# Attention and gated layer in one kernel: no MoE unit in a pair's step, its first product in another PSUM bank

## The chip, the cores and the metric

One core of a Trainium2 chip runs the whole program. The metric is device time in microseconds of one execution, the median of three runs. TensorE (PE) multiplies and transposes, VectorE (DVE), ScalarE (ACT) and GpSimd (POOL) do the rest, SyncE (SP) issues nearly all transfers. Each engine works through its own instructions in the order in which they were written.

## The reference

Everything is fp32. Attention of 4 batches x 8 heads x 576 positions x 64 with rotated q and k is followed by a layer "x @ w_in, relu, a convolution of three taps along the sequence, sigmoid gate, @ w_out", called MoE in the code.

```python
q_rot, k_rot = (rotate(q), rotate(k))
scores = scale * np.matmul(q_rot, k_rot.transpose(0, 1, 3, 2))
attn = np.exp(scores - np.max(scores, axis=-1, keepdims=True))
attn = attn / (np.sum(attn, axis=-1, keepdims=True) + 1e-09)
x = np.matmul(attn, v)                      # heads side by side: 4 x 576 x 512
h = np.maximum(x @ w_in, 0.0)               # 512 -> 1024
conv_out = sum(conv_w[k] * hp[:, k:k + S, :] for k in range(3))
out = (h * (1.0 / (1.0 + np.exp(-conv_out)))) @ w_out
```

## The kernel before

The order of the work is written out by hand: every engine executes in the order in which the loop over steps `n` emits. Heads go in 16 pairs `p`; a pair takes five steps, `n = 5p + s`. In step `n`:

- **S** (`emit_S`, L251): the scores of one block of 128 query rows for both heads, into the PSUM tiles `sp` (two buffers). VectorE takes the maxima (L259), ScalarE the exponentials (L263) into `st`, or `str` for the short fifth block.
- **T** (`emit_T`, L311): the transposes of the block of the step before, into the two PSUM buffers `tp` (`t_tile`); ScalarE copies them to `pt` (L189). Blocks 0 to 3 fill columns 0 to 511 of `pt`, the fifth (10 transposes, called T4 here) columns 512 to 575.
- **R** (`emit_Trem`, L336): remaining columns, in steps `n % 5 == 2` and `4`, also in a `tp` buffer, copied by VectorE (L191).
- **E** (`emit_E`, L367): the product with V, all of it in the steps `n % 5 == 0` (called pair steps), one part per half `j`. Half 0 reads columns 0 to 289 of `pt`, half 1 columns 286 to 575. `spare` gives each a `tp` buffer; ScalarE copies it to `xn` (L377).
- `emit_rinv` (L344 to 354): reciprocal of the sums, through DRAM into `rb`; `norms` (L381) multiplies `xn` by it, then `xT` is made in two parts (L385 ScalarE, L386 GpSimd).

From step `WIDE = 26` on, MoE units are put between these. The 2304 positions are 8 blocks of 288. **M1** (`emit_M1`, 12 matmuls, L400) is one eighth of a block's first product, in a buffer of the PSUM pool `m` (two buffers, `pm`); then come relu (L408 ACT), convolution (L412, L414 DVE), tanh (L420 ACT), gate (L423 DVE), and a split in two parts (L431 ACT, L432 POOL) into `g`. `defer` puts these a number of ticks (units on PE) later. **M2** (`emit_M2`, 6 matmuls, L478) is a quarter of the second product for 128 positions; its `pm` buffer is held over four units, then VectorE copies it to `ot` (L485) and SyncE stores it (L488).

The table `moe` says which unit goes into which step. A block's units get a place x in 0 to 1; a step holds as much of that as its entry of `room` says. Before, a block has `MB = 10` steps, and a pair step has half the room of another. Transfers are in the same table: rank 19 puts `load` and `load_v` at the end of a step, behind its units, those of V (`vm`, `vr`) and of k into steps `n % 5 == 3`. After the last step two blocks are left for the tail, in which `m_tile` has other buffers.

Of the kernel before, what the change touches and what calls it, by code (L numbers as in the profile page):

```python
# [20 lines left out]
def attention_moe_kernel(ctx, tc, q, k, v, w_in, conv_w, w_out, tab, tabx, out):  # L21
# [3 lines left out]
    NP = B * NPB  # L25
# [3 lines left out]
    NF = DFF // 128  # L29
# [4 lines left out]
    STEPS = 5  # L34
# [5 lines left out]
    psum = {}  # L40
# [39 lines left out]
    def defer(k, fn, rank=1):  # L80
        due.setdefault(slot[0] + k, []).append((rank, len(due.get(slot[0] + k, [])), fn))
# [6 lines left out]
    def t_tile():  # L88
        return psum["t"].tile([128, 512], F32, tag="t", name="tp")

    def after(fn):
        if "m" in psum or late["n"] + 1 == WIDE:
            fn()
        else:
            at(late["n"] + 1, 0.35, fn)

    def spare(n):
        a = free["at"]
        if "m" in psum or late["n"] + 1 == WIDE:
            return t_tile()[:, 0:n]  # L100
        assert a + n <= 960
        free["at"] = a + n
        return free["ps"][:, a:a + n]

    def m_tile():
        if late["tail"]:
            return psum["t"].tile([128, 512], F32, tag="mt", name="mt")
        return psum["m"].tile([128, 512], F32, tag="m", name="pm")
# [131 lines left out]
    def go(d, key):  # L240
        for fn in d.pop(key):
            fn()
# [89 lines left out]
    def emit_Trem(p, first, num):  # L332
        ps = spare(128 * num)
        for u in range(num):
            x = ST[p, first + u].rearrange("p h k -> p (h k)")[:, 512:640]
            nc.tensor.transpose(ps[:, 128 * u:128 * u + 128], x, idf)  # L336
        after(lambda: evac("V", pt[:, 8, 128 * first:128 * (first + num)], ps))
# [19 lines left out]
    norms = {}  # L357
# [2 lines left out]

    def emit_E(p, j, a=0, n=XW):
        b, hp = divmod(p, NPB)
        xp = spare(n)
        o = (S - XW) * j
        for i in range(5):
            for h in range(2):
                nc.tensor.matmul(  # L367
                    out=xp[64 * h:64 * h + 64, :],
                    lhsT=vmain[p][:, h, i, :] if i < 4 else vrem[:, h, :],
                    rhs=pt[:, 2 * i + h if i < 4 else 8, o + a:o + a + n],  # L370
                    start=(i == 0),
                    stop=(i == 4),
                )
        if a == 0:
            xns[p, j] = p2.tile([128, XW], F32, tag="xn", name="xn", bufs=4)
        xn = xns[p, j]
        after(lambda: nc.scalar.activation(out=xn[:, a:a + n], in_=xp, func=AF.Copy))  # L377

        def norm():
            sl = xslot[b, hp, j] = free_slots.pop(0)  # L380
            nc.vector.tensor_tensor(out=xn, in0=xn, in1=rb[p][:, o:o + XW], op=ALU.mult)  # L381

        def split():
            sl = xslot[b, hp, j]
            nc.scalar.activation(out=xT[:, sl, 0, :], in_=xn, func=AF.Copy)  # L385
            nc.gpsimd.tensor_tensor(out=xT[:, sl, 1, :], in0=xn, in1=xT[:, sl, 0, :].bitcast(F32), op=ALU.subtract)  # L386

        norms[p, j] = lambda: (norm(), defer(1, split))
# [194 lines left out]
    def m2_units(blk):  # L583
        tiles = list(range(HS * blk // 128, HS * (blk + 1) // 128))
        return [lambda t=t, i=i: emit_M2(t, i) for t in tiles for i in range(4)]
# [8 lines left out]
    WIDE = 26  # L594
    MB = 10
# [4 lines left out]
    def at(n, rank, fn):  # L600
        plan.setdefault(n, []).append((rank, len(plan.get(n, [])), fn))

    def emit():
        with tc.manual_schedule(engines=engines):
# [17 lines left out]
            for p in range(1, NP):  # L622
                n = STEPS * p
# [6 lines left out]
            for p in range(NP):  # L630
                n = STEPS * p
                for s in range(STEPS):
                    m = n + s
                    first = m < WIDE
                    if m:
                        at(m - 1 if first else m, 0.5 if first else 0, lambda p=p, s=s: emit_S(p, s))
                    at(m, 0.2, lambda p=p, s=s: go(reds, (p, s)))
                    at(m, 0.3 if first else 1.5, lambda p=p, s=s: go(exps, (p, s)))
                    for h in range(2 if s < 4 else 1):
                        at(m + 1, 0 if m + 1 < WIDE else 1, lambda p=p, s=s, h=h: emit_T(p, s, h))  # L640
                if n + 4 < WIDE:
                    for i in range(4):
                        at(n + 1 + i, 2, lambda p=p, i=i: emit_Trem(p, i, 1))
                else:
                    for i in range(2):
                        at(n + 2 + 2 * i, 2, lambda p=p, i=i: emit_Trem(p, 2 * i, 2))
                if n + 8 < WIDE:
                    for i in range(4):
                        at(n + 5 + i, 4, lambda p=p, i=i: emit_E(p, i // 2, XW // 2 * (i % 2), XW // 2))
                else:  # L650
                    for i in range(2):
                        m = n + 5 + (i if n + 5 < WIDE else 0)
                        at(m, 4 if m < WIDE else 10, lambda p=p, i=i: emit_E(p, i))
                at(n + 5, 4.5, lambda p=p: emit_rinv(p))
                for j in range(2):
                    at(n + (9 if j and n + 8 < WIDE else 8), 1.7 + j, lambda p=p, j=j: norms.pop((p, j))())
            nw = len(wsteps)
            for i, u in enumerate(wsteps):
                x = (WIDE - 1) * i // nw
# [2 lines left out]
            at(14, 2, turn_cw)  # L662
            moe = {}
            for blk in range(2 * B - 2):
                n0 = WIDE + MB * blk
                room = [0.5 if n % STEPS == 0 and n < STEPS * NP + 2 else 1.0 for n in range(n0, n0 + MB)]
                us = [(0.09 + 0.1 * f, lambda blk=blk, f=f: emit_M1(blk, f)) for f in range(NF)]
                if blk:
                    m2 = m2_units(blk - 1)
                    ne = 4 if blk % 4 == 0 else 0  # L670
                    us += [(0.05 * i if i < ne else 0.05 * ne + (1 - 0.05 * ne) * (i - ne) / (len(m2) - ne), u) for i, u in enumerate(m2)]
                for x, u in us:
                    y, k = x * sum(room), 0
                    while y >= room[k]:
                        y -= room[k]
                        k += 1
                    moe.setdefault(n0 + k, []).append((x, u))
# [56 lines left out]
            for u in seq + second + m2_units(last) + m2_units(LASTB):  # L734
                u()
                tick()

    emit()


# [48 lines left out]
```

## Time and profile before

| what | value |
|---|---|
| three runs | 515.56, 516.81, 519.25 us; median 516.81 |
| the profiled execution | 514.66 us, of it the span 512.7 |
| PE busy | 469.0 us (91%), 3880 matmuls |
| DVE, ACT, POOL busy | 365.0 (71%), 311.8 (61%), 300.3 us (59%) |
| granted TensorE clock | 0.983 on the mean of the span; 1.00 in every stretch from 128 us on |
| chain that ended last | PE 67%, DVE 13%, ACT 7%, POOL 5%, DMA 5% |

PE is busy to nine tenths or more in nearly each slice from step 26 (about 128 us) on. A busy share of an engine does not say whether a wait of PE ends on it; this is read from the waits, step by step. A pair step can be found in the timeline of PE by its ten transposes of `str`; a step begins with eight matmuls into `sp`.

### The profile page before, as it was taken

Reading aid. Unit: us, or ns where it says so; the run is one execution under the profiler, and the core shown is the slowest. Engines: PE = TensorE matmul, PEld = TensorE weight load, DVE = VectorE, ACT = ScalarE, POOL = GpSimd, SP = SyncE. Lnnn points to the kernel's source line nnn. Section 1 sums busy time; section 2 is a strip of 40 time slices with the busy share of each in tenths; the row PEclk is TensorE's granted clock in tenths of the full one; section 3 lists DMA queues with packets and bytes.
Section 4 is the critical chain, followed back from the end, with each engine's and each line's share of the span. In section 5 each row is a group of like instructions: output and inputs, shape, how many; then the busy total and the mean of one; then the engine's idle time right before and its main releaser. Section 6 shows DMA issues by size and latency. Waiting matters only on the chain.

```text
span 512.7 us, 10801 instructions
## 1 busy us (share of the span) xinstructions
PE 469.0 (91%) x3880; PEld 350.0 (68%) x3880; DVE 365.0 (71%) x656; ACT 311.8 (61%) x821; POOL 300.3 (59%) x479
## 2 busy tenths in 40 slices
PE   1878789786999899999999999999999999999997
PEld 1445446553766587767878687868777676889986
DVE  5699889995597759684868487765868284748951
ACT  2588877885576767675667575754657564325520
POOL 3789988999576747646492829274573021314530
PEclk9999987997999999999999999999999999999999
DMA  8978965843424243433425251524220201000011
GB/s 225 178 128 165 191 158 140 188 113 76 88 47 94 47 93 68 93 69 73 90 49 90 63 100 45 88 73 88 51 68 1 68 1 46 22 21 22 1 42 60
DMA packets 139256, 42.61 MB, mean 83 GB/s; under 512 B 132012, under 2 KB 132804, under 8 KB 139204
## 3 DMA queue, kind: packets, MB, share of 16 engines
q1 hardware_dynamic: 137860, 41.54, 37.1%
q8 instruction: 30, 0.49, 0.4%
q10 hardware_dynamic: 1344, 0.39, 0.3%
q14 instruction: 22, 0.18, 0.1%
HBM read 37.12 MB, written 4.79 MB: 82 GB/s over the span
## 4 chain that ended last, share of the span: by engine, by line
PE 67%; DVE 13%; ACT 7%; POOL 5%; DMA 5%; issue 2%; SPq 0%; ACTq 0%; DVEq 0%; POOLq 0%
PE pm L400 13%; PE sp L251 12%; PE pm L478 11%; PE tp L367 11%; PE mt L478 8%; PE mt L400 5%; PE tp L311 5%; DVE negm L259 4%; ACT st L263 3%; ACT pt L189 2%; DMA rq<-q 2%; POOL rk L180 1%; DVE c L414 1%; POOL woutl L559 1%; DMA rk<-k 1%
## 5 line engine op out<-in xcount | busy, mean ns | idle before, releaser
L259 DVE TENSOR_REDUCE negm<-sp 128x1 f32<-128x576 f32 x144 | 102.4, 747 | 73.9 <-PE sp L251 66.6
L432 POOL TENSOR_TENSOR g<-c,g 128x288 fp32r<-128x288 f32 (+4 forms) x88 | 56.8, 658 | 154.6 <-ACT g L431 151.7
L189 ACT ACTIVATE pt<-tp 128x512 f32<-128x512 f32 (+3 forms) x176 | 84.4, 528 | 53.7 <-PE tp L311 53.3
L251 PE MATMUL sp<-kT,qT 64*128 64x288 f32 (+4 forms) x556 | 104.3, 474 | 6.4 <-DVE kT L227 3.2
L263 ACT ACTIVATE st<-sp,negm 128x576 f32<-128x576 f32 x128 | 94.0, 746 | 14.6 <-DVE negm L259 14.1
L400 PE MATMUL pm<-xT,winh 128*128 128x290 f32 x384 | 81.7, 305 | 0.0
L414 DVE SCALAR_TENSOR_TENSOR c<-rr,cw,c 128x288 f32<-128x288 f32 x128 | 77.6, 606 | 4.5
L251 PEld LDWEIGHTS sp<-kT,qT 64*128 64x128 f32 (+1 forms) x556 | 47.2, 179 | 33.5 <-issue 15.4
L478 PE MATMUL pm<-wouth,g 128*128 128x512 f32 x176 | 65.8, 415 | 0.0
L400 PEld LDWEIGHTS pm<-xT,winh 128*128 128x128 f32 x384 | 62.3, 189 | 3.2 <-issue 0.4
L311 PEld LDWEIGHTS tp<-idf,st 64*128 64x128 f32 x1024 | 42.5, 140 | 27.1 <-ACT st L263 16.2
L180 POOL TENSOR_TENSOR rq<-rq,tabt 128x192 f32<-128x192 f32 x90 | 56.8, 666 | 5.5 <-DMA rq<-q 5.3
L311 PE MATMUL tp<-idf,st 64*128 64x64 f32 x1024 | 49.4, 229 | 10.5 <-ACT st L263 10.4
L400 PE MATMUL pm<-xT,winl 128*128 128x290 f32 x192 | 56.7, 296 | 0.0
L367 PE MATMUL tp<-pt,vm 128*64 128x290 f32 x384 | 53.6, 422 | 3.4 <-ACT pt L189 3.4
L180 POOL TENSOR_TENSOR rk<-rk,tabt 128x192 f32<-128x192 f32 x90 | 56.6, 665 | 0.0
L423 DVE SCALAR_TENSOR_TENSOR c<-c,rr 128x288 f32<-128x288 f32 x64 | 36.6, 575 | 15.3 <-ACT c L420 15.3
L412 DVE TENSOR_SCALAR c<-rr,cw 128x288 f32<-128x288 f32 x64 | 33.3, 521 | 18.0 <-ACT rr L408 14.0
L386 POOL TENSOR_TENSOR xT<-xn,xT 128x290 fp32r<-128x290 f32 x32 | 29.6, 940 | 24.1 <-ACT xT L385 24.1
L367 PEld LDWEIGHTS tp<-pt,vm 128*64 128x64 f32 x384 | 27.0, 140 | 23.0 <-ACT pt L189 4.4
L420 ACT ACTIVATE c<-c 128x288 f32<-128x288 f32 x64 | 28.5, 445 | 17.7 <-DVE c L414 17.5
L478 PEld LDWEIGHTS pm<-wouth,g 128*128 128x128 f32 x176 | 33.0, 188 | 8.1
(102 smaller groups left out, 797.8 us busy)
## 6 DMA issues: line engine op xcount, KB each, us to landing
out<-ot SPq DMA_DIRECT2D x17, 256.0 KB
rq<-q SPq DMA_DIRECT2D x30, 144.0 KB
rq<-q SPq DMA_DIRECT2D x60, 72.0 KB
rk<-k SPq DMA_DIRECT2D x30, 144.0 KB
rk<-k SPq DMA_DIRECT2D x60, 72.0 KB
w<-moe_w_in SPq DMA_DIRECT2D x8, 512.0 KB
vm<-v SPq DMA_DIRECT2D x32, 128.0 KB
w<-moe_w_out SPq DMA_DIRECT2D x8, 512.0 KB
```

The costliest lines, as they stand in the source:

```text
L180: nc.gpsimd.tensor_tensor(out=y, in0=y, in1=tabt[:, a:a + 3], op=ALU.mult)
L189: nc.scalar.activation(out=out, in_=in_, func=AF.Copy, scale=1.0 if sc is None else sc)
L251: nc.tensor.matmul(out=out, lhsT=qt[64 * h:64 * h + 64, c], rhs=kt[64 * h:64 * h + 64, a:a + n], start=True, stop=True)
L259: reds.setdefault((p, s), []).append(lambda: nc.vector.tensor_reduce(out=nm, in_=sc, axis=AX.XY if len(sc.shape) == 3 else AX.X, op=ALU.ma ...
L263: lambda: nc.scalar.activation(out=dst, in_=sc, func=AF.Exp, bias=nm, scale=1.0, accum_out=sm)
L311: nc.tensor.transpose(ps[r][:, 64 * k:64 * k + 64], x[i], idf[i, i])
L367: nc.tensor.matmul(out=xp[64 * h:64 * h + 64, :], lhsT=vmain[p][:, h, i, :] if i < 4 else vrem[:, h, :], rhs=pt[:, 2 * i + h if i < 4 else ...
L400: nc.tensor.matmul(out=ps[:, 0:XW], lhsT=w[:, kk, fs], rhs=xT[:, xs, e, :], start=(i == 0), stop=(i == n - 1))
L414: nc.vector.scalar_tensor_tensor(out=c, in0=r[:, j + e:j + e + HS], scalar=cw[:, 8 * e + f:8 * e + f + 1], in1=c, op0=ALU.mult, op1=ALU.add,)
L423: nc.vector.scalar_tensor_tensor(out=c, in0=c, scalar=1.0, in1=r[:, j + 1:j + 1 + HS], op0=ALU.add, op1=ALU.mult)
L432: nc.gpsimd.tensor_tensor(out=lo, in0=c[:, o:o + n], in1=hi.bitcast(F32), op=ALU.subtract)
L478: nc.tensor.matmul(out=ops[tt][:, 0:width], lhsT=g_tile(tt, f, e), rhs=w[:, f, cols], start=(f == 0 and i == 0), stop=(f == NF - 1 and i = ...
```

## The change

Four edits, all of them in the order of the work:

1. `emit_E`: from step 26 on half 0 of a pair's product takes a buffer of the pool `m` (`pm`), half 1 a `tp` buffer as before.
2. `norms` (for pairs whose product lies in step 26 or later) one step earlier, in step `n + 7` of a pair instead of `n + 8`.
3. `room` is 0 in pair steps (up to step 80) and 1 in all others; a block's units have the eight other steps, and each block after the first starts two steps earlier.
4. Units are spread evenly by their number over these steps, and M1 comes ahead of M2 in a step.

By the table that results, steps 26 to 28 and 31 to 33 have one M1 still, step 29 two, and all others between 34 and 83 that are not pair steps an M1 and an M2 (the eight steps of block 4, in 64 to 73, two or three units in another mix). Steps 30, 40, 50, 60 and 70 lose the one M1 that they had; steps 35, 45, 55, 65 and 75 had none before. The last unit ahead of the tail is in step 83 instead of 84; the number of units is the same.

```diff
     def emit_E(p, j, a=0, n=XW):
         b, hp = divmod(p, NPB)
-        xp = spare(n)
+        xp = m_tile()[:, 0:n] if "m" in psum and j == 0 else spare(n)
...
                 for j in range(2):
-                    at(n + (9 if j and n + 8 < WIDE else 8), 1.7 + j, lambda p=p, j=j: norms.pop((p, j))())
+                    at(n + (9 if j else 8) if n + 8 < WIDE else n + 8 - (n + 5 >= WIDE), 1.7 + j, lambda p=p, j=j: norms.pop((p, j))())
...
             for blk in range(2 * B - 2):
-                n0 = WIDE + MB * blk
-                room = [0.5 if n % STEPS == 0 and n < STEPS * NP + 2 else 1.0 for n in range(n0, n0 + MB)]
-                us = [(0.09 + 0.1 * f, lambda blk=blk, f=f: emit_M1(blk, f)) for f in range(NF)]
+                n0 = WIDE + MB * blk - (MB - NF if blk else 0)
+                room = [float(n % STEPS != 0 or n > STEPS * NP) for n in range(n0, n0 + (MB if blk else NF))]
+                us = [((f + 0.5) / NF, lambda blk=blk, f=f: emit_M1(blk, f)) for f in range(NF)]
                 if blk:
                     m2 = m2_units(blk - 1)
                     ne = 4 if blk % 4 == 0 else 0
-                    us += [(0.05 * i if i < ne else 0.05 * ne + (1 - 0.05 * ne) * (i - ne) / (len(m2) - ne), u) for i, u in enumerate(m2)]
-                for x, u in us:
-                    y, k = x * sum(room), 0
+                    us += [(0.05 * i if i < ne else 0.05 * ne + (1 - 0.05 * ne) * (i - ne + 0.5) / (len(m2) - ne), u) for i, u in enumerate(m2)]
+                us.sort(key=lambda e: e[0])
+                for i, (x, u) in enumerate(us):
+                    y, k = (i + 0.5) / len(us) * sum(room), 0
                     while y >= room[k]:
```

**PE around a pair step without a unit.** Before, the end of step 44 and step 45 (R is L336, S is L251, T4 is L311 with `str`, E is L367):

```order
L478 MATMUL pm<-wouth,g 128x512
L336 MATMUL tp<-idf,st 128x128 x2
L251 MATMUL sp<-kT,qT 128x288 x4
L311 MATMUL tp<-idf,str_82 128x64 x10
L367 MATMUL tp<-pt,vm 64x290 x8
L367 MATMUL tp<-pt,vr 64x290 x2
L367 MATMUL tp<-pt,vm 64x290 x8
L367 MATMUL tp<-pt,vr 64x290 x2
```

After, the same place (the end of an M1, then R, an M2, and the pair step):

```order
L400 MATMUL pm<-xT,winl 128x290
L336 MATMUL tp<-idf,st 128x128 x2
L478 MATMUL pm<-wouth,g 128x512
L478 MATMUL pm<-woutl,g 128x512
L478 MATMUL pm<-wouth,g 128x512 x2
L478 MATMUL pm<-woutl,g 128x512
L478 MATMUL pm<-wouth,g 128x512
L251 MATMUL sp<-kT,qT 128x288 x4
L311 MATMUL tp<-idf,str_83 128x64 x10
L367 MATMUL pm<-pt,vm 64x290 x8
L367 MATMUL pm<-pt,vr 64x290 x2
L367 MATMUL tp<-pt,vm 64x290 x8
```

An M2 now stands between R and the pair step, and half 0 of E goes to `pm`.

**DVE in the steps that follow an M1.** Before, the three steps behind a pair step (`n % 5` of 1, 2 and the maxima of 3; L259 are the maxima of S):

```order
L259 TENSOR_REDUCE negm<-sp 128x1 x2
L224 STREAM_TRANSPOSE qT<-rq 128x576
L259 TENSOR_REDUCE negm<-sp 128x1 x2
L412 TENSOR_SCALAR c<-rr_1702,cw 128x288
L414 SCALAR_TENSOR_TENSOR c<-rr_1702,cw,c 128x288 x2
L191 COPY pt<-tp 128x256
L423 SCALAR_TENSOR_TENSOR c<-c,rr_1702 128x288
L259 TENSOR_REDUCE negm<-sp 128x1 x2
```

After, the same three steps:

```order
L259 TENSOR_REDUCE negm<-sp 128x1 x2
L224 STREAM_TRANSPOSE qT<-rq 128x576
L412 TENSOR_SCALAR c<-rr_1703,cw 128x288
L414 SCALAR_TENSOR_TENSOR c<-rr_1703,cw,c 128x288 x2
L259 TENSOR_REDUCE negm<-sp 128x1 x2
L381 TENSOR_TENSOR xn<-xn,rb 128x290
L191 COPY pt<-tp 128x256
L381 TENSOR_TENSOR xn<-xn,rb 128x290
L423 SCALAR_TENSOR_TENSOR c<-c,rr_1703 128x288
L412 TENSOR_SCALAR c<-rr_1704,cw 128x288
L414 SCALAR_TENSOR_TENSOR c<-rr_1704,cw,c 128x288 x2
L259 TENSOR_REDUCE negm<-sp 128x1 x2
```

The convolution of an M1 (L412, L414), and the gate of the M1 before it (L423), now stand ahead of the next step's maxima; before, the maxima stood first.

**SP between two pair steps.** Before (the last of the loads of q, those of V, the first of k, the last of k, and the store):

```order
L141 DMA rq<-q 32x18x32
L151 DMA vm<-v 128x4x64
L152 DMA vr<-v 64x64
L151 DMA vm<-v 128x4x64
L152 DMA vr<-v 64x64
L139 DMA rk<-k 32x18x64
...
L141 DMA rk<-k 32x18x32
L488 DMA out<-ot 128x512
L349 DMA rd<-rt 9x32 x4
```

After:

```order
L141 DMA rq<-q 32x18x32
L488 DMA out<-ot 128x512
L151 DMA vm<-v 128x4x64
L152 DMA vr<-v 64x64
L151 DMA vm<-v 128x4x64
L152 DMA vr<-v 64x64
L139 DMA rk<-k 32x18x64
...
L141 DMA rk<-k 32x18x32
L349 DMA rd<-rt 9x32 x4
```

The store of an M2 tile, which waits for its copy on VectorE, is now ahead of V's loads; before, it was behind them and those of k.

## Rows read from the trace of the kernel before

**Rows 1.** Waits of PE from 128 us on: total us, times, longest.

```profile
PE tp L367 <- ACT pt L189: 2.9, 6, 0.5
PE tp L336 <- ACT pt L189: 2.5, 2, 1.5
PE sp L251 <- ACT st L263: 1.9, 3, 0.7
PE tp L311 <- DVE pt L191: 1.6, 3, 0.6
```

**Rows 2.** PE timeline, pair step 45: start, length, work, idle ahead of it.

```profile
226.54 1.39 PE L251 MATMUL sp<-kT,qT 64*128 64x288 f32 x8
...
228.45 0.53 PE L311 MATMUL tp<-idf,str 64*128 64x64 f32 x9 [0.52 <-DVE pt L191]
229.45 2.17 PE L367 MATMUL tp<-pt,vm 128*64 128x290 f32 x16 [0.47 <-ACT pt L189]
...
234.48 1.24 PE L251 MATMUL sp<-kT,qT 64*128 64x288 f32 x8
```

**Rows 3.** PE timeline, starts of step 49, pair step 50 and step 51.

```profile
249.31 1.19 PE L251 MATMUL sp<-kT,qT 64*64 64x288 f32 x8
...
254.50 1.24 PE L251 MATMUL sp<-kT,qT 64*128 64x288 f32 x8
...
262.81 1.24 PE L251 MATMUL sp<-kT,qT 64*128 64x288 f32 x8
```

**Rows 4.** PE timeline, starts of step 54, which has an M2 alone, and step 55.

```profile
277.64 1.19 PE L251 MATMUL sp<-kT,qT 64*64 64x288 f32 x8
...
281.21 1.39 PE L251 MATMUL sp<-kT,qT 64*128 64x288 f32 x8
```

**Rows 5.** PE timeline, starts of pair step 35 and of step 36.

```profile
171.75 1.83 PE L251 MATMUL sp<-kT,qT 64*128 64x288 f32 x7
...
179.83 0.51 PE L251 MATMUL sp<-kT,qT 64*128 64x288 f32 x2
```

**Rows 6.** DVE timeline, step 47: maxima, convolution, gate, with GpSimd idle.

```profile
240.62 1.42 DVE L259 TENSOR_REDUCE negm<-sp 128x1 f32<-128x576 f32 x2 [2.77 <-PE sp L251]
241.96 0.36 DVE L412 TENSOR_SCALAR c<-rr,cw 128x288 f32<-128x288 f32 x1
242.36 1.07 DVE L414 SCALAR_TENSOR_TENSOR c<-rr,cw,c 128x288 f32<-128x288 f32 x2
...
244.01 0.46 DVE L423 SCALAR_TENSOR_TENSOR c<-c,rr 128x288 f32<-128x288 f32 x1 [0.24 <-ACT c L420]
```

**Rows 7.** DVE timeline, step 49: a convolution beside GpSimd, and the copy of an M2 tile.

```profile
251.72 0.92 DVE L412 TENSOR_SCALAR c<-rr,cw 128x288 f32<-128x288 f32 x1
252.68 1.17 DVE L414 SCALAR_TENSOR_TENSOR c<-rr,cw,c 128x288 f32<-128x288 f32 x2
253.77 0.68 DVE L485 TENSOR_SCALAR ot<-pm 128x512 f32<-128x512 f32 x1
```

**Rows 8.** POOL timeline at the same time.

```profile
250.68 1.79 POOL L386 TENSOR_TENSOR xT<-xn,xT 128x290 fp32r<-128x290 f32 x2 [2.22 <-ACT xT L385]
```

**Rows 9.** ACT timeline, steps 47 to 49: an exponential, a relu, a tanh.

```profile
242.80 0.76 ACT L263 ACTIVATE st<-sp,negm 128x576 f32<-128x576 f32 x1
...
249.42 0.41 ACT L408 ACTIVATE rr<-pm 128x289 f32<-128x289 f32 x1 [0.26 <-PE pm L400]
249.82 0.44 ACT L420 ACTIVATE c<-c 128x288 f32<-128x288 f32 x1
```

**Rows 10.** SP timeline, steps 47 to 50: first and last load of V, the store.

```profile
242.24 0.44 SPq L151 DMA_DIRECT2D vm<-v  x1
...
243.99 0.47 SPq L152 DMA_DIRECT2D vr<-v  x1
...
254.47 0.37 SPq L488 DMA_DIRECT2D out<-ot  x1
```

**Rows 11.** Busy time by stretch just after V's loads: last two columns DMA share, GB/s.

```profile
245.50:246.50 1.00, 1.00 (x20) 0.87 (x17) 0.79 (x2) 0.30 (x1) 0.00 (x0) 1.00 0.01 1
```

## The prediction

> **What bounds the kernel now.** I read the busy shares first: PE is at nine tenths or more in almost every slice from step 26 on, so there the time is PE's work plus what PE waits. The work is the same before and after, instruction for instruction, and the granted clock is already full; only waits, and slow stretches that the waits table does not list, can come or go. So I read the waits of PE next [rows 1]: 8.9 us in all after 128 us. VectorE's copy of R ahead of T4 is 1.6, ScalarE's copies to `pt` ahead of E are 2.9 and ahead of R 2.5, and S waits 1.9 for exponentials. Then I looked in PE's timeline for where they fall: in pair steps without a unit [rows 2], and not in one with a unit [rows 3].
>
> The reader should see the two stalls of step 45 [rows 2]. R is the last unit of step 44, so only S lies between it and T4, and T4 waits 0.52 for the buffer that VectorE is still copying. Then T4 holds both `tp` buffers, so half 0 of E waits 0.47 for ScalarE to empty one, though it reads none of the columns that T4 fills.
>
> **What a pair step costs.** Step 49 (S, T, M2, R, M1) takes 254.50 - 249.31 = 5.19 us [rows 3], step 54, the same without M1, 281.21 - 277.64 = 3.57 [rows 4]; an M1 is 1.62. Pair step 50 with an M1 takes 8.31 [rows 3], so a pair step's own work is 8.31 - 1.62 = 6.69. Step 45 took 234.48 - 226.54 = 7.94 [rows 2]: 1.25 more, of which the stalls show 0.99 and 0.26 is hidden in matmuls that start late. Step 35 took 8.08 [rows 5], 1.39 more, of which 0.47 is a listed wait, so 0.92 is hidden.
>
> **Edit 1 and edits 3 and 4, on PE.** Half 0 of E in `pm` waits only for the relu of the last M1, which emptied that buffer: 0.41 us [rows 9], in the step before. Half 1 needs T4's copies and has half 0 ahead of it as cover, half of the 5.03 us from 229.45 to 234.48 [rows 2], so 2.5. That takes the six waits of E, 2.9. With an M2 between R and the pair step, R's copy has that M2 besides S as cover; the three waits of T4, 1.6, go. The hidden parts go with them: 0.92 in step 35, and 0.26 each in steps 45, 55, 65 and 75, 1.04. Taking the M1 out of steps 30, 40, 50, 60 and 70 costs nothing as long as these covers hold; if one did not, each such step would pay up to the 1.25 of step 45. Of the two waits of R, the one in step 34 (2.5 - 1.5 = 1.0) came with no unit between T and R; now an M1 lies there. The one of 1.5 is in step 79, where ScalarE's copies stood behind other work of its own; there I leave 0.3. The 1.9 of S are in steps 28, 29 and 32; what S follows there is the same as before, and they stay.
>
> Sum: 2.9 + 1.6 + 1.0 + 1.2 + 0.92 + 1.04 = 8.7 us.
>
> **Edit 4, on VectorE and ScalarE.** M1 first means that its convolution is written ahead of the next step's maxima. Before, VectorE stood idle 2.77 us until S was done and took the maxima at once [rows 6]. Now the maxima wait for the convolution, it waits for the gate before it and for the relu, and the relu stands behind this step's exponentials. Where a tanh and a gate lie between too, which is so from step `n % 5 == 2` to the next, a loop closes over one step: relu 0.41, tanh 0.44 [rows 9], gate 0.46, convolution 0.36 + 1.07, two maxima 1.42 [rows 6], the last exponential 0.76 [rows 9], 4.92 together. Step 49's 5.19 [rows 3] is longer, so nothing is lost. With GpSimd beside it a convolution took 0.92 + 1.17 [rows 7, 8], and the loop is 5.58: 0.39 over the step. There are 9 such places (steps 37 to 77, every fifth), so the cost lies between 0 and 3.5 us. GpSimd's work beside it is short (1.79 us, [rows 8]), and the loop meets fewer maxima in the step that follows; I take 1.4.
>
> The row shows 0.92 for L412 beside GpSimd and 0.36 without [rows 6, 7]. The Trainium skill (SBUF — State Buffer, section Who interferes with whom) says that VectorE and GpSimd share a pair of ports, which VectorE takes for an instruction with two inputs in SBUF and for some with one, a `tensor_scalar` among them, and that one of the two then waits. That speaks against this change, since the convolution now stands ahead of something that PE waits for. By that rule each of the 9 places would pay the 0.39, and the sum would be 3.5 instead of 1.4.
>
> **Edit 2 and the queues.** The norm is one step earlier. It needs `rb`, two rounds of transfers that depend on each other. V's four loads took 3.3 us from the first issue to the last byte (242.24 to before 245.5, [rows 10, 11]); twice that is 6.6. From the reciprocal late in the pair step (some 4 us into 6.69) to the norm behind the maxima of the second step after it there are 2.7 + 5.2 + 2.7 = 10.6. Nothing. On SP the store of an M2 tile is now ahead of V's loads in 8 steps (38, 43, 48, 53, 58, 63, 73, 78). It waits for the copy, 0.68 [rows 7], behind the M2 that ends the step. Then the store's issue of 0.37, V's four issues (242.24 to 244.46) and the last bytes 1.04 later [rows 10, 11] make 0.68 + 0.37 + 2.22 + 1.04 = 4.3 us from the end of step 48. E needs V in step 50 after S and T4, 5.19 + 1.4 = 6.6 us from there (228.45 - 226.54 - 0.52 = 1.4, [rows 2, 3]). The slack is 2.3; I cost it at nothing. On GpSimd only the order of short pieces changes.
>
> **Result.** 8.7 - 1.4 = 7.3 us. The profiled execution took 514.66, so it would take 507.4. It is 0.4% below the median of the three runs, 516.81, from which the same gain leads to 509.5. I forecast **508.4**, the middle.
>
> **Rivals.**
>
> *The loop costs the gain* (0.18). The 0.39 falls on two steps of each five, since the gate also stands ahead of the convolution one step later, and on S's own lateness besides: 18 x 0.39 = 7.0. Left are 1.7 us, 513.0 on the profiled execution's time, 515.1 on the median's. For it: S already waits three times for exponentials [rows 1], with only two `sp` buffers. Against it: a pair step has no M1 behind it and lets everything catch up.
>
> *Only half of the stalls go* (0.13). E's waits go, but T4 still waits for something of VectorE or ScalarE, since these now run later into the step: 2.9 + 1.0 + 1.2 less 1.4 = 3.7, hence 511.0 or 513.1. For it: T4 also needs the exponentials of the short block, which now stand behind a convolution. Against it: an M2 and S, some 2.5 us, lie between.
>
> *V comes late* (0.08), slower. Place: the first matmul of E in the 8 pair steps named above. The store holds V's loads back in SP's queue, and its bytes may go ahead of theirs. It decides where V's last byte is more than 2.3 us later than the 4.3 that I worked out, so 6.6 us after the M2's end. If it is 8.6, each of the 8 waits 2.0: 16 - 7.3 = 8.7 slower, 523.4 on the profiled execution's time. For it: in the trace of before V's loads are landed 9 us before pair step 50 begins (245.5 against 254.50, [rows 3, 11]), so nothing shows how a short lead works. Against it: the numbers above.
>
> **How the numbers follow.** Forecast 0.61, rivals 0.18, 0.13 and 0.08. A measurement of this kernel can tell about 1% from no change. Faster by over 1% (below 511.6) are the forecast nearly whole (0.60) and half of the second rival (0.06): 0.66. Within 1%: 0.26. Slower: 0.08. The low end is the whole 8.7 with nothing lost, from 514.66: 506.0, and I go to 505.5 for a wait of S that might go too. The high end is the first rival on the median's time, 515.5. What lies above, V late and some of the first rival, is under 2 in 10.
>
> **What would show it.** In the profile after: the rows of PE waiting for `pt` L189 ahead of E and for L191 ahead of T4 are gone; pair steps take 6.7 us from S to S, all alike; steps with M1 and M2 stay at 4.9 to 5.2. The loop shows as S waiting for `st` L263, or as such steps above 5.3. V late shows as E waiting for a transfer of v. The forecast is wrong if PE's idle time in the stretch of two-unit steps grows, or if pair steps take over 7.5 us.

## The result and the profile after

The changed kernel takes **504.24 us** (median of 6 runs, 503.52 to 504.97), the kernel before, on the same chip, 515.55 (515.22 to 519.25). The ratio is 0.9766, 95% interval 0.9738 to 0.9794: faster by 2.3%. The forecast of 508.4 had the right side, but the time lies below its range of 505.5 to 515.5. The profiled execution took 504.07 us with a span of 502.3; before, 514.66 and 512.7. The spans differ by 10.4 and the medians by 11.3, where I had forecast 7.3.

The page of the kernel after, part 1: busy time, share of the span and instructions of each engine.

```profile
PE 467.1 (93%) x3880; PEld 348.5 (69%) x3880; DVE 366.9 (73%) x656; ACT 310.3 (62%) x821; POOL 300.7 (60%) x479
```

The waits of PE from 128 us on in the kernel after (total, times, longest; compare [rows 1]):

```profile
PE sp L251 <- ACT st L263: 2.3, 3, 1.4
```

Four rows, 8.9 us, have become one. Every wait of E, T4 and R is gone; S still waits three times, in steps 28, 32 and 34. PE's timeline of pair step 50 in the kernel after:

```profile
253.38 1.24 PE L251 MATMUL sp<-kT,qT 64*128 64x288 f32 x8
254.45 0.47 PE L311 MATMUL tp<-idf,str 64*128 64x64 f32 x10
254.85 2.17 PE L367 MATMUL pm<-pt,vm 128*64 128x290 f32 x16
...
259.89 0.76 PE L251 MATMUL sp<-kT,qT 64*128 64x288 f32 x4
```

From S to the next S it takes 259.89 - 253.38 = **6.51 us**, and so do all ten pair steps from 30 to 75; I had worked out 6.69. From S to E it is 254.85 - 253.38 = 1.47, where step 45 of before took 229.45 - 226.54 = 2.91 [rows 2]. These 1.44 us are the whole excess of step 45 (7.94 - 6.51 = 1.43), although its two listed waits come to 0.99. A listed wait begins at the modelled end of the matmul before; but matmuls overlap (those of M2, of 0.40 us, start 0.24 apart in the fourth experiment), so here a stop cost more, from start to start, than its row says.

Where the 10.4 us went, by the starts of the steps in both traces:

| stretch | before, us | after, us | gain |
|---|---|---|---|
| up to step 26, no instruction differs | 127.41 | 126.81 | 0.6 |
| steps 26 to 28, no instruction differs | 15.45 | 16.90 | -1.4 |
| steps 29 to 35 | 36.96 | 36.65, of it 3.02 for an M1 and an M2 that came later before | 3.3 |
| steps 36 to 78, the same work | 238.90 | 233.11 | **5.8** |
| step 79 to the end | 94.00, of it those 3.02 | 88.82 | 2.2 |

The 1.4 in steps 26 to 28 is no effect of the change: S of step 28 waited 1.35 where it had waited 0.63, and behind that wait the granted clock fell to 0.51 from 139.20 to 142.70 us (the last section), while the trace of before has 1.00 there. From step 29 on, where the kernels differ, the gain is 11.3.

In steps 36 to 78 the eight pair steps give 6.2: they took 64.72 together, and now 8 x 6.51 with the four M1 that left them (4 x 1.62), 58.56. The other steps there are 0.4 longer.

### The profile page after: what moved, and what is told of

It reads as the page before. It is cut to its first block, busy times and chain, and to the rows that moved or that the text cites. A ratio compares the mean times of both kernels' runs of the same rounds, so it can differ in the third digit from the quotient of the medians.

```text
span 502.3 us, 10752 instructions
## 1 busy us (share of the span) xinstructions
PE 467.1 (93%) x3880; PEld 348.5 (69%) x3880; DVE 366.9 (73%) x656; ACT 310.3 (62%) x821; POOL 300.7 (60%) x479
## 4 chain that ended last, share of the span: by engine, by line
PE 71%; DVE 9%; DMA 6%; POOL 6%; ACT 4%; issue 2%; SPq 2%; ACTq 0%; DVEq 0%; POOLq 0%
PE pm L400 15%; PE sp L251 13%; PE pm L478 12%; PE mt L478 8%; PE pm L367 6%; PE tp L367 5%; PE mt L400 5%; PE tp L311 5%; DVE negm L259 3%; DMA w<-moe_w_out 2%; ACT st L263 2%; POOL rk L180 2%; POOL woutl L559 1%; DMA rk<-k 1%; ACT pt L189 1%
## 5 line engine op out<-in xcount | busy, mean ns | idle before, releaser
L259 DVE TENSOR_REDUCE negm<-sp 128x1 f32<-128x576 f32 x144 | 102.2, 745 | 36.7 <-PE sp L251 29.1
L189 ACT ACTIVATE pt<-tp 128x512 f32<-128x512 f32 (+3 forms) x176 | 84.1, 526 | 63.4 <-PE tp L311 62.6
L432 POOL TENSOR_TENSOR g<-c,g 128x288 fp32r<-128x288 f32 (+4 forms) x88 | 56.9, 658 | 96.5 <-ACT g L431 95.2
L251 PE MATMUL sp<-kT,qT 64*128 64x288 f32 (+4 forms) x556 | 104.1, 480 | 5.9 <-DVE kT L227 2.5
L414 DVE SCALAR_TENSOR_TENSOR c<-rr,cw,c 128x288 f32<-128x288 f32 x128 | 81.3, 635 | 4.5
L400 PE MATMUL pm<-xT,winh 128*128 128x290 f32 x384 | 84.0, 311 | 0.1
L251 PEld LDWEIGHTS sp<-kT,qT 64*128 64x128 f32 (+1 forms) x556 | 46.2, 181 | 37.7 <-issue 12.8
L386 POOL TENSOR_TENSOR xT<-xn,xT 128x290 fp32r<-128x290 f32 x32 | 27.9, 883 | 69.3 <-ACT xT L385 69.3
L478 PE MATMUL pm<-wouth,g 128*128 128x512 f32 x176 | 64.2, 406 | 0.0
L180 POOL TENSOR_TENSOR rq<-rq,tabt 128x192 f32<-128x192 f32 x90 | 58.0, 676 | 6.1 <-DMA rk<-k 6.1
L311 PEld LDWEIGHTS tp<-idf,st 64*128 64x128 f32 x1024 | 43.2, 142 | 25.7 <-ACT st L263 14.5
L311 PE MATMUL tp<-idf,st 64*128 64x64 f32 x1024 | 49.9, 231 | 9.2 <-ACT st L263 9.2
L423 DVE SCALAR_TENSOR_TENSOR c<-c,rr 128x288 f32<-128x288 f32 x64 | 37.7, 591 | 21.9 <-ACT c L420 21.9
L412 DVE TENSOR_SCALAR c<-rr,cw 128x288 f32<-128x288 f32 x64 | 31.1, 485 | 26.3 <-ACT rr L408 21.6
L400 PEld LDWEIGHTS pm<-xT,winl 128*128 128x128 f32 x192 | 36.9, 192 | 0.0
L478 PE MATMUL pm<-woutl,g 128*128 128x512 f32 x88 | 34.7, 395 | 0.0
```

What stands on the lines that cost most here:

```text
L180: nc.gpsimd.tensor_tensor(out=y, in0=y, in1=tabt[:, a:a + 3], op=ALU.mult)
L189: nc.scalar.activation(out=out, in_=in_, func=AF.Copy, scale=1.0 if sc is None else sc)
L251: nc.tensor.matmul(out=out, lhsT=qt[64 * h:64 * h + 64, c], rhs=kt[64 * h:64 * h + 64, a:a + n], start=True, stop=True)
L259: reds.setdefault((p, s), []).append(lambda: nc.vector.tensor_reduce(out=nm, in_=sc, axis=AX.XY if len(sc.shape) == 3 else AX.X, op=ALU.ma ...
L311: nc.tensor.transpose(ps[r][:, 64 * k:64 * k + 64], x[i], idf[i, i])
L400: nc.tensor.matmul(out=ps[:, 0:XW], lhsT=w[:, kk, fs], rhs=xT[:, xs, e, :], start=(i == 0), stop=(i == n - 1))
```

## The experiments

All ratios are to the kernel before on the same chip; the kernel after stands at 0.9766, and 0.01 is 5.2 us. What is said in us against the kernel after is the difference of two ratios and uncertain by 2 to 3 us; the steps of the traces are sharper.

**Edit 1 alone**, in the kernel before:

```diff
-        xp = spare(n)
+        xp = m_tile()[:, 0:n] if "m" in psum and j == 0 else spare(n)
```

> The kernel before with edit 1 alone (half 0 of E in an `m` buffer; the units stay where they were). Theory (the terms of the forecast, each from its rows): the waits of E for ScalarE's copies, 2.9 us, go; T4 still waits 1.6 us for VectorE's copy, and pair steps with an M1 still take 8.3 us. That gives 515.6 - 2.9 = 512.7, ratio 0.994. Rival 1: all of the excess of a pair step without a unit (1.1 to 1.6 us in steps 35, 45, 55, 65, 75 over the 6.51 that every pair step takes after the change, 7.0 in all) belonged to E; then 508.6, ratio 0.986. Rival 2: what E no longer waits, T4 or half 1 of E waits instead; then 515, ratio 1.0, with rows of PE waiting for `pt` L189 as before.

515.39 us, ratio 0.9964 (0.9939 to 0.9989): 1.9 us gained. PE's waits from 128 us on:

```profile
PE pm L367 <- ACT rr L408: 1.9, 1, 1.9
PE tp L311 <- DVE pt L191: 1.6, 3, 0.6
```

E no longer waits for L189, and T4's row has stayed, as the theory said; S's (2.6) and R's rows, not shown, have stayed too. But a new row has come: in pair step 70, which holds an M1, E waits 1.9 for that M1's relu. So steps 45, 55, 65 and 75 are shorter by 0.54 to 0.56 each, and step 70 is longer by 1.9; this trace also has two stretches of 3.5 us at a granted clock of 0.51, in steps 28 and 35, where the trace of before has 1.00. Pair step 45 of this run, on PE:

```profile
228.75 1.39 PE L251 MATMUL sp<-kT,qT 64*128 64x288 f32 x8
229.83 0.22 PE L311 MATMUL tp<-idf,str 64*128 64x64 f32 x1
230.65 0.52 PE L311 MATMUL tp<-idf,str 64*128 64x64 f32 x9 [0.51 <-DVE pt L191]
231.10 2.17 PE L367 MATMUL pm<-pt,vm 128*64 128x290 f32 x16
```

From S to E it is now 2.35. So E's wait, listed as 0.47, had cost 2.91 - 2.35 = 0.56, and T4's, listed as 0.51, costs 2.35 - 1.47 = 0.88: its first transpose was out at 229.83, and the next started 0.82 later instead of some 0.05.

**All but edit 1**, in the kernel after:

```diff
-        xp = m_tile()[:, 0:n] if "m" in psum and j == 0 else spare(n)
+        xp = spare(n)
```

> The kernel after with half 0 of E back in a `tp` buffer, all else as after. Theory: in every pair step T4 holds both `tp` buffers and half 0 waits some 0.5 us for ScalarE to empty one (0.47 in step 45 of before), now in 11 to 14 pair steps, since none has a unit in it as a cover: 504.2 + 5.5 to 7 = 509.7 to 511, ratio 0.989 to 0.991 to the kernel before. Rival: the gain comes from where the units lie; then 504 to 505.5, ratio 0.978 to 0.981.

511.75 us, ratio 0.9898 (0.9852 to 0.9943), 6.8 us over the kernel after. Each of the ten pair steps takes 7.10. PE's wait for those copies, and then pair step 50:

```profile
PE tp L367 <- ACT pt L189: 7.2, 11, 2.0
```

```profile
257.13 0.47 PE L311 MATMUL tp<-idf,str 64*128 64x64 f32 x10
258.12 2.18 PE L367 MATMUL tp<-pt,vm 128*64 128x290 f32 x16 [0.52 <-ACT pt L189]
```

T4 does not wait, E does, every time. So the table of units cures T4 and edit 1 cures E, and edit 1 is worth 1.9 us on the old table and 6.8 on the new one, which has no M1 as a cover there.

**M2 ahead of M1.** Where an M1 and an M2 have the same place x, the order of writing decides. This turns it round, and the loop over the convolution is taken apart.

```diff
+                us = us[NF:] + us[:NF]
                 us.sort(key=lambda e: e[0])
```

> The kernel after with M2 ahead of M1 in the steps that have both (the order of the kernel before there), so that the convolution no longer stands ahead of the next step's maxima by the length of an M2. It takes apart the loop of 1.4 us that the forecast charged. Theory (the loop forms but costs PE nothing): no gain, 504.2 with 1 us on either side; steps with M1 and M2 stay at 4.9 to 5.2 us. Rival 1 (the loop costs what was forecast, hidden in late starts of matmuls): 1.4 less, 502.8. Rival 2 (M1 first is itself worth something, as relu, tanh and gate begin earlier): 1 to 4 us more, with waits of M2 or of the norm's users.

509.23 us, ratio 0.9846 (0.9809 to 0.9883): 4.1 us slower than the kernel after, rival 2 in size. But not in the place of the loop: from pair step 35 to step 76 it takes 399.72 - 174.98 = 224.74, the kernel after 398.60 - 173.85 = 224.75. There the loop costs **nothing**. The loss is behind: from step 79 to the end 93.2 us against 88.8. PE's waits in this kernel from 398 us on, where the kernel after has none:

```profile
PE mt L478 <- ACT g L431: 1.3, 1, 1.3
PE tp L336 <- ACT pt L189: 0.8, 1, 0.8
PE sp L251 <- ACT st L263: 0.5, 1, 0.5
PE mt L478 <- POOL g L432: 0.2, 1, 0.2
```

With M2 first, `g` and the copies of T come out late where the last steps run into the tail. M1 first, which I had only charged, earns there; the rows of R and M2 are 2.3 of the 4.4. Behind M2's wait of 1.3 the granted clock fell, with PE busy throughout (columns as in the last section):

```profile
443.70:447.20 3.50, 3.50 (x14) 3.35 (x14) 0.69 (x1) 0.14 (x1) 0.00 (x0) 0.51 0.20 75
```

Where the kernel after has 1.00 in its tail until the last 1.3 us, these 3.5 us cost about 3.5 x 0.49 = 1.7 more, an estimate; with the 2.3 that is 4.0 of the 4.4.

**M1 between S and T**, in 18 steps (in one of them, step 73, the first unit is an M2), with S's exponentials ahead of T's copies there as before:

```diff
-   at(m, 0.3 if first else 1.5, lambda p=p, s=s: go(exps, (p, s)))
+   at(m, 0.3 if first else 0.9 if m > 35 and m % 5 in (1, 3) else 1.5, lambda p=p, s=s: go(exps, (p, s)))
...
                 for e in evs:
+                    if e[0] == 1 and n > 35 and n % 5 in (1, 3) and not done:
+                        ms[0]()
+                        tick()
+                        done = 1
```

> The kernel after with the first unit, M1, between S and T instead of behind T in the 18 steps after step 35 with n % 5 of 1 or 3. PE's work is the same, but it changes over between the tiled matmuls (64 rows or columns) and the full ones twice more in each. In the trace of the kernel after an M1 between T4 and E takes 1.81 us, elsewhere 1.62. Theory (the 0.19 is the price of changing over there and back): 18 x 0.19 = 3.4 us more, 507.6, ratio 0.984, with these steps at 5.07 instead of 4.88. Rival 1 (the price belongs to the place between T4 and E alone): 504.2, ratio 0.978. Rival 2 (T's copies, now later, hold up what follows): 1 us or more in each such step, above 515, with rows of PE waiting for `pt` L189 or for `tp`.

511.39 us, ratio 0.9890 (0.9857 to 0.9923): 6.4 us slower, with no new wait in these steps. Those with two units take 5.22 instead of 4.88, those with three 0.34 to 0.36 more as well, but for step 68 (0.03). From step 36 to step 79 it is 239.05 against 233.11, 5.9. That is the theory's mechanism at twice its price. PE in step 48 of the kernel after, then of this one:

```profile
243.30 1.24 PE L251 MATMUL sp<-kT,qT 64*128 64x288 f32 x8
244.37 0.66 PE L311 MATMUL tp<-idf,st 64*128 64x64 f32 x16
244.96 0.54 PE L400 MATMUL pm<-xT,winh 128*128 128x290 f32 x2
...
246.69 0.40 PE L478 MATMUL pm<-wouth,g 128*128 128x512 f32 x1
246.93 0.40 PE L478 MATMUL pm<-woutl,g 128*128 128x512 f32 x1
```

```profile
245.49 1.24 PE L251 MATMUL sp<-kT,qT 64*128 64x288 f32 x8
246.66 0.54 PE L400 MATMUL pm<-xT,winh 128*128 128x290 f32 x2
...
248.48 0.71 PE L311 MATMUL tp<-idf,st 64*128 64x64 f32 x16
249.12 0.50 PE L478 MATMUL pm<-wouth,g 128*128 128x512 f32 x1
249.46 0.39 PE L478 MATMUL pm<-woutl,g 128*128 128x512 f32 x1
```

After, S and T (both tiled) stand together and M1 and M2 (both 128*128) too. Here M1 lies between two tiled groups: 0.10 more ahead of it (1.17 against 1.07), 0.09 behind (1.82 against 1.73), then 0.05 more in T (0.64 against 0.59) and 0.10 at M2's first matmul (0.34 against 0.24). These are two changes of tiling more, 0.17 each on the mean. Between T4 and E there is a change anyway (64*128 to 128*64), so an M1 there adds one: 8.31 - 6.51 - 1.62 = 0.18. My 0.19 for "there and back" was the price of one. A rival is that the number format costs it, since S, T and E work on fp32 and M1 and M2 on fp32r. But in step 49 of the kernel after, the format changes twice among 128*128 matmuls: M1's last starts at 251.53, R's two transposes (fp32) from 251.67 on, M2's second matmul at 252.12. Of these 0.59 us, 0.13 are M1's and 0.24 M2's; 0.22 are left for two transposes of 128 columns, where those of T, of 64 columns, follow each other by 0.05 to 0.06. So nothing is left for the change of format. The Trainium skill (TensorEngine Tiling (Array Packing), section Tiling Modes) says that changing the tiling mode drains TensorE; these rows agree, at 0.17 a change.

**Without edit 2**, the norm a step later again:

```diff
-   at(n + (9 if j else 8) if n + 8 < WIDE else n + 8 - (n + 5 >= WIDE), 1.7 + j, lambda p=p, j=j: norms.pop((p, j))())
+   at(n + (9 if j else 8) if n + 8 < WIDE else n + 8, 1.7 + j, lambda p=p, j=j: norms.pop((p, j))())
```

> The kernel after without edit 2: the first norm of each pair a step later again, at n + 8. Theory (the forecast charged edit 2 at nothing, and gave it nothing): 504.2 with 1 us on either side, ratio 0.978, no new wait of PE. Rival 1 (with the units spread from two steps earlier, the first M1 of a block now needs the earlier norm): PE waits for xT in steps 34, 44, 54, ..., 0.5 to 2 us each, 2 to 10 us more. Rival 2 (the earlier norm stands in the way of something on VectorE): some 1 us less.

507.61 us, ratio 0.9854 (0.9828 to 0.9880): 4.5 us slower; the theory is refuted. It is not rival 1 either, since PE never waits for xT. Pair steps 40, 45, 60 and 65 take 7.0 to 7.3, 50 and 55 take 6.7: 2.9 us together, of the 4.0 by which this trace is longer. Another 1.3 lies behind step 79, where R waits 0.5 and M2 0.4; there the cause was not traced. VectorE ahead of pair step 40 in this kernel, then the last exponential and PE's S:

```profile
194.53 0.78 DVE L381 TENSOR_TENSOR xn<-xn,rb 128x290 f32<-128x290 f32 x2
195.24 0.68 DVE L485 TENSOR_SCALAR ot<-pm 128x512 f32<-128x512 f32 x1
195.84 0.78 DVE L423 SCALAR_TENSOR_TENSOR c<-c,rr 128x288 f32<-128x288 f32 x1
196.54 0.91 DVE L412 TENSOR_SCALAR c<-rr,cw 128x288 f32<-128x288 f32 x1
197.49 1.71 DVE L414 SCALAR_TENSOR_TENSOR c<-rr,cw,c 128x288 f32<-128x288 f32 x2
199.12 0.74 DVE L259 TENSOR_REDUCE negm<-sp 128x1 f32<-128x576 f32 x1
```

```profile
199.90 0.74 ACT L263 ACTIVATE str<-sp,negm 128x576 f32<-128x576 f32 x1 [1.83 <-DVE negm L259]
```

```profile
200.08 1.70 PE L251 MATMUL sp<-kT,qT 64*128 64x288 f32 x7
```

From the norm to the short block's maximum it is 4.59 us. In the kernel after the norm lies a step earlier, and the same chain from L485 on takes 2.75 (195.53 to 198.28), here 3.88: gate and convolution, beside GpSimd's part of `xT` (195.50, 1.78), take 0.78, 0.91 and 1.71 where they take 0.43, 0.35 and 1.50. So the maximum comes late, the exponential starts 0.18 ahead of S instead of 1.28 (199.06 and 200.34) and ends at 200.64, and the second head's half of S needs that `sp` buffer. The listed waits of PE show nothing of it, only the stretched row of S (1.70 for seven matmuls against 1.24 for eight).

**The short S made to need two buffers**, to see whether slack had swallowed the loop:

```diff
             ps = psum["s"].tile([128, 2, 512], F32, tag="s", name="sp")
+            also = psum["s"].tile([128, 2, 512], F32, tag="s", name="sp")
+            mm(also[0:64, 0, 0:64], 0, 64, 64, c)
```

> The kernel after with one matmul of 64 columns more in each S of a short block (n % 5 = 4), into a second `sp` buffer which nothing reads; so this S needs both buffers of the step before, where it needed one. Theory (the loop of 5.9 us over the steps with a gate and a convolution is absorbed here, since the short S needs only one buffer: in step 49 S began at 248.19, and the exponential in the other buffer ended at 248.27): S in the 10 steps from 34 to 79 waits 0.1 to 0.4 us for the last exponential, and the added matmul takes about 0.1; 2 to 5 us more, 506 to 509, ratio 0.982 to 0.988, with rows of PE waiting for `st` L263. Rival (there is slack enough without it): only the added matmul, 1 to 1.5 us, 505.5, ratio 0.980, no such row.

509.18 us, ratio 0.9880 (0.9854 to 0.9906), 5.9 over the kernel after, at the theory's upper end; from pair step 35 to step 76, free of the early steps' scatter, 228.18 against 224.75, 3.4. Step 44 of this run on PE:

```profile
224.92 0.33 PE L251 MATMUL sp<-kT,qT 64*64 64x64 f32 x2
225.64 1.19 PE L251 MATMUL sp<-kT,qT 64*64 64x288 f32 x8 [0.40 <-ACT st L263]
...
230.83 0.51 PE L251 MATMUL sp<-kT,qT 64*128 64x288 f32 x2
```

The step takes 230.83 - 224.92 = 5.91, where it is 5.19 in the kernel after. Steps 39, 59 and 64 grow by 0.6 to 0.7 as well, 49 and 54 by 0.2, and 69 and 74 by 0.1, about what the added matmul takes. So the loop is real, and in the kernel after the short block takes it up.

**An M1 put back into 8 pair steps**, edit 3 undone by itself:

```diff
+            early = [(f + 0.5) / NF for f in range(1, NF)]
...
+            for n in range(WIDE + 10, STEPS * NP, STEPS):
+                e = min(moe[n], key=lambda e: e[0])
+                if e[0] in early and n - 1 not in moe:
+                    moe[n].remove(e)
+                    moe[n - 1] = [e]
```

> The kernel after with an M1 put back between T4 and E in 8 pair steps (40 to 65, 75 and 80 or so, taken from the step behind, which keeps its M2), so edit 3 undone by itself. Theory (each change of PE between tiled and full matmuls costs 0.17 to 0.18; T4 to E is one already, with an M1 between them there are two): these pair steps take 6.51 + 1.62 + 0.18 = 8.31, the steps behind 4.88 - 1.62 = 3.26, so 8 x 0.18 = 1.4 us more, 505.7, ratio 0.980. Rival 1: E's half 0, now in an `m` buffer, waits for the relu of an M1 just before (1.85 us in step 70 of the run with edit 1 alone): 0.3 to 1.9 us in each, 508 to 520, with rows of PE waiting for rr L408. Rival 2: no measurable difference, 504.2, pair steps at 8.13.

**533.63 us, ratio 1.0349** (1.0322 to 1.0376): 30 us over the kernel after and slower than the kernel before, beyond even rival 1. The M1 lie in pair steps 35 to 60, 70 and 75. PE's wait in front of E, then ScalarE and PE in pair step 50:

```profile
PE pm L367 <- ACT rr L408: 13.2, 7, 2.2
```

```profile
268.98 0.73 ACT L263 ACTIVATE st<-sp,negm 128x576 f32<-128x576 f32 x1
...
269.69 0.41 ACT L408 ACTIVATE rr<-pm 128x289 f32<-128x289 f32 x1
```

```profile
267.99 0.29 PE L400 MATMUL pm<-xT,winl 128*128 128x290 f32 x1
270.15 3.86 PE L367 MATMUL pm<-pt,vm 128*64 128x290 f32 x16 [1.87 <-ACT rr L408]
```

M1's last matmul starts at 267.99, its relu stands behind both exponentials, and E starts as the relu ends. An M2 tile is held over four units, so one of the two `m` buffers is often taken; then E's half 0 needs the buffer of the M1 just ahead. Only in step 70 of the eight it did not wait, and there the step took 8.32.

**The same with half 0 in a `tp` buffer**, edits 1 and 3 both undone in these steps:

```diff
-        xp = m_tile()[:, 0:n] if "m" in psum and j == 0 else spare(n)
+        xp = spare(n)
```

> As x7_m1_in_pair_step (an M1 back between T4 and E in 8 pair steps), but with half 0 of E in a `tp` buffer as before: edits 1 and 3 both undone there. It parts the 29 us of that run: E's wait for the relu of the M1 just before it (listed 13.2 us in 7 places), and what came behind (steps n % 5 = 2 at 5.8 instead of 5.1, with S waiting 0.64 for exponentials, and the step before at 3.96 instead of 3.26). Theory (edit 1 is what makes an M1 in a pair step dear: with the M2 tile still open, E's half 0 gets the buffer of that very M1): pair steps 8.31, the steps behind catch up to 3.3 and 5.1, 505 to 508 with the 7 pair steps' share of waits, ratio 0.980 to 0.985; the three pair steps without an M1 wait 0.5 each for T4's copies. Rival (the M1's relu and convolution, now behind the pair step's exponentials, delay the steps after it whatever buffer E takes): 0.7 + 0.7 stay in each of 7 places, 515 to 518, ratio 1.0.

519.32 us, ratio 1.0047 (1.0007 to 1.0086). The pair steps with an M1 take 8.32, so the other 15.6 us of the run before were E's wait for the relu and what hung on it. But what came behind has stayed, as the rival said. Steps 51 and 52:

```profile
267.99 1.24 PE L251 MATMUL sp<-kT,qT 64*128 64x288 f32 x8
...
271.94 1.24 PE L251 MATMUL sp<-kT,qT 64*128 64x288 f32 x4 [0.63 <-ACT st L263]
```

Step 51, with one unit, takes 3.96 instead of 4.88 - 1.62 = 3.26, and step 52 5.80 instead of 5.08, with S waiting: 1.4 in each of seven places, 10 of the 14.5 us over the kernel after. Of the rest, 1.4 are the theory's 8 x 0.18, and 3.2 lie in pair steps 30, 65 and 80, where half 0 waits for T4's copies as in the second experiment. So a step with a single unit is shorter here than what ScalarE and VectorE need for its block. Steps 31 to 33 of the kernel after, with one M1 each, show the same (3.96 in step 31).

**Units earlier.** Could that slack in steps 26 to 33 be filled?

```diff
-   n0 = WIDE + MB * blk - (MB - NF if blk else 0)
+   n0 = WIDE + MB * blk - (MB - NF + 1 if blk else 0)
...
-   for n in range(n0, n0 + (MB if blk else NF))]
+   for n in range(n0, n0 + (MB if blk else NF - 1))]
```

> The kernel after with block 0's eight M1 in seven steps instead of eight, and every later block a step earlier. The last stretch then has some two units less. In steps 26 to 34 of the kernel after PE has waits of S (2.3 us listed) and steps of 3.9 to 5.7 us with one M1, of which S, T and M1 are 3.5; a second M1 there would be partly free. Theory: the last stretch loses 2 units, about 3 us, steps 26 to 33 get 1 to 2 longer; 502.5 to 503.5, ratio 0.974. Rival (VectorE and ScalarE, with another relu, tanh, gate and convolution, set the pace there): the steps grow by all of it, 504 to 506.

508.98 us, ratio 0.9849 (0.9812 to 0.9887): 4.3 slower than the kernel after, more than the rival said. Steps 26 to 35 take 2.5 more for an M1 and an M2 more (3.0). But the kernel after has 3.5 us at a granted clock of 0.51 in step 28, and this trace has 1.00 there; without that, an estimated 1.7 us, the steps grew by about 4, so on the whole none of the slack was filled. And from step 36 to step 76 it is 220.98 against 218.24, and S waits 0.3 to 0.6 in the steps `n % 5 == 4` from 39 to 64, where the kernel after just does not:

```profile
PE sp L251 <- ACT st L263: 5.7, 9, 1.1
```

VectorE's copy of an M2 tile (0.69), which the kernel after makes behind the maxima of step 48 (248.30), stands ahead of gate and convolution here, a step earlier (220.68 in step 38), and the maxima start 3.64 behind the start of S (224.21 - 220.57) instead of 2.67 (245.97 - 243.30). So the slack of the short step was used up by one more piece of work on VectorE.

> The same by two steps: block 0's M1 in six steps (two M1 in steps 26, 28 and 31), later blocks two steps earlier. In step 42 the first M1 of block 2 then comes in the step of that batch's last norm. Theory: the last stretch loses 3 units, about 4.6 us; steps 26 to 33 get 2 to 3 longer; 502 to 503, ratio 0.973. Rival 1 (VectorE and ScalarE set the pace in steps 26 to 33): 504 to 507. Rival 2 (M1 waits for xT in steps 42 and 62, 1 to 2 us each): 505 to 508, with such rows of PE.

Two steps earlier gave 504.46 us, ratio 0.9765 (0.9727 to 0.9803). In it the first M1 of block 2 reads `xT` 3 us before it is written (218.8 against 222.1), so it leaves out a wait that it needs, and its time shows only that nothing is to be won this way. No kernel here beats the kernel after.

## Why the prediction fell short

**Which waits go, and that no others come: right.** E, T4 and both rows of R are gone, S's stay, pair steps are alike.

**The size of a pair step's excess: the step that failed first.** I took the pair step's own work as 8.31 - 1.62 = 6.69, with an M1 at the price it has between other full matmuls. Between T4 and E it costs 1.80, the change of tiling included, and the floor is 6.51. So three things were short by 0.18 each time: the hidden part in steps 45, 55, 65 and 75 (I took 0.26), step 35's, and edit 3, "costs nothing", which saves 0.18 for each of five M1. For the eight pair steps from 40 to 75 my terms were 4 x 0.47 for E, 1.6 for T4 and 4 x 0.26, 4.5 in all; measured 6.2.

**The loop on VectorE and ScalarE: mis-sized, 1.4 where it is 0.** Its length was nearly right: 5.87 us from the relu of step 47 to that of step 48 in the kernel after (242.38 to 248.25), where I had 5.58. DVE there:

```profile
243.18 0.46 DVE L423 SCALAR_TENSOR_TENSOR c<-c,rr 128x288 f32<-128x288 f32 x1 [0.38 <-ACT c L420]
243.55 0.97 DVE L412 TENSOR_SCALAR c<-rr,cw 128x288 f32<-128x288 f32 x1
244.56 1.49 DVE L414 SCALAR_TENSOR_TENSOR c<-rr,cw,c 128x288 f32<-128x288 f32 x2
245.97 1.42 DVE L259 TENSOR_REDUCE negm<-sp 128x1 f32<-128x576 f32 x2
...
249.27 0.36 DVE L412 TENSOR_SCALAR c<-rr,cw 128x288 f32<-128x288 f32 x1
249.67 1.07 DVE L414 SCALAR_TENSOR_TENSOR c<-rr,cw,c 128x288 f32<-128x288 f32 x2
```

The maxima come 1.4 us late, the second exponential runs to 248.27, but S of step 49 starts on time at 248.19, since the short block takes one `sp` buffer. I compared the loop with step 49 (5.19), though it lies over steps 47 and 48 (5.08 and 4.89), which made it look shorter against PE than it is, and I did not ask which buffer the next S needs. The 1.17 that I took for L414 beside GpSimd was not a reading of [rows 8] either: that piece had ended at 252.47, and L414 began at 252.68. With two buffers the loop bites (the sixth experiment), without the loop nothing is gained (the third). The rule that I weighed, of the Trainium skill (SBUF — State Buffer, section Who interferes with whom), holds on the first rows: L412 and L414 take 0.97 and 1.49 beside GpSimd's part of `xT` (243.55, 1.62). In the next step L412 takes 0.36 with GpSimd idle, and L414 1.07 though GpSimd's L432 runs beside it; there it is L432 that takes longer, 1.55, where it took 0.94 with no convolution beside it in the third experiment (240.13). PE did not wait in either place, and the rival built on the rule is refuted.

**Edit 2, "nothing": half right.** V's last load is issued at 251.22 and E starts at 254.85 without a wait, as I worked out:

```profile
251.22 0.47 SPq L152 DMA_DIRECT2D vr<-v  x1
```

But I had asked only if the norm's inputs were there in time. That it frees VectorE and ScalarE in the steps ahead of the pair step is worth 2.9 us in six pair steps, and 4.5 us in all (the fifth experiment); the forecast contained that without knowing it, which was luck.

**Edits 3 and 4: more than I saw.** "If a cover did not hold, up to 1.25 a step" was too little: with edit 1, an M1 in a pair step costs up to 2.2 of wait and 1.4 behind it. The second rival (T4 still waits) and the third (V late) did not come.

**The sum.** The 11.3 us from step 29 on exceed the 7.3 by 1.7 of the eight pair steps, 1.0 of the loop (1.4 less the 0.4 by which the other steps grew), and 1.4 of the other terms: for steps 34, 35, 79 and 80 I had 4.1, and the stretches in which they lie gained 3.3 + 2.2. Of that 1.4, 0.55 is step 30 (8.68 before, 6.51 + 1.62 after), from which I expected nothing; the rest stays open. I had also taken the granted clock as full, and so as no term at all. In the profiled execution it fell once, in step 28, and with the wait ahead of it took 1.4 back; with the 0.6 before step 26, which stays open too, that leaves the 10.4. Both stretches hold the same instructions in both kernels, and step 26 began between 126.55 and 127.66 in all these runs, so a single pair of profiles can be off by that much.

## What to carry to other kernels

Take the cost of a stall from start to start against the same step without it, not from the listed wait, and measure a step's floor where its matmuls stand in the order that the change gives them, since moving a full matmul between tiled ones costs two changes of tiling. Before charging a late engine, ask which buffer the next matmul needs: slack in one short step took up a loop in every five. Edits that share a buffer or a cover have no price of their own; try each with and without the others.

## What the runs showed of the hardware

In step 50 of the run with an M1 put back and half 0 in `pm`, PE stood idle for 1.85 us and then ran E at the lower clock. Windows of that run (columns: stretch, its length, busy time of PE, PEld, DVE, ACT, POOL, granted clock, DMA share, GB/s):

```profile
268.30:270.15 1.85, 0.00 (x0) 0.00 (x0) 1.60 (x4) 1.85 (x6) 1.71 (x5) 1.00 0.13 13
270.15:273.80 3.65, 3.65 (x16) 1.89 (x18) 2.64 (x4) 0.28 (x1) 3.65 (x7) 0.53 0.04 9
273.90:276.80 2.90, 2.90 (x26) 1.52 (x22) 0.00 (x0) 0.41 (x1) 1.36 (x3) 1.00 0.24 86
```

The granted clock is 0.53, close to 1.2 of 2.4 GHz, for 3.65 us and then full again; half 0 of E took 4.18 (274.33 - 270.15) where it took 2.49 in step 45, and step 50 11.94 where step 45 had 10.59 with a longer wait (2.20) and a clock of 1.00 behind it. The kernel after shows the same once, behind the wait of S in step 28 (1.35, up to 137.99):

```profile
139.20:142.70 3.50, 3.50 (x28) 2.90 (x25) 3.31 (x7) 1.49 (x5) 0.00 (x0) 0.51 0.00 0
```

So a stop of this kind can cost once more in what follows it, and does not always; two traces are to be compared only with the granted clock of each stretch beside them.

Nor do the starts of tiled matmuls always keep the written order: in pair step 40 of the run without edit 2, where the second head's half of S waited, T4's first transposes start at 201.38 and S's last matmul, which is written ahead of them, at 201.62.
